# A written order of steps, moved up to batch 1's subtraction: where loads, maxima, transposes and query fetches stand

## The chip, the cores and the metric

The kernel runs on one core of a Trainium2 chip. Its time is the device time of one execution in microseconds (us); the time of a kernel is the median of its runs. Five engines run their own instruction streams in order and wait for each other through semaphores: TensorE (PE in the profile, with PEld for its weight loads), VectorE (DVE), ScalarE (ACT), GpSimd (POOL) and SyncE (SP), which here issues the DMAs.

## The reference, cut to what matters

Eight batches of 576 tokens pass through an attention over 32 memory slots (8 heads of 64) and then through a mixture of 8 experts in which each token goes to one expert:

```
a = exp(phi - max_tokens(phi));  a /= sum_tokens(a) + 1e-9
k_m = einsum('bhsm,bhsd->bhmd', a, k);  v_m = einsum('bhsm,bhsd->bhmd', a, v)
attn = softmax(q @ k_m.T / sqrt(64));   x = attn @ v_m        # 576 x 512 per batch
logits = x @ w_gate;  local = sigmoid(x @ w_local)
# token 0 takes its own best expert; a later token keeps its predecessor's
# expert e unless local < 0.5, then it takes its own best one
out = softmax(logits)[e] * (relu(x @ w1[e]) @ w2[e])          # w1 512 x 1024, w2 1024 x 512
```

## The kernel before

For each batch the expert of token 0 (the *choice*, L1023 to L1025) is found at run time, and this expert's W1 and W2 are loaded and applied to all 576 tokens; the few tokens that have another expert are done again in a loop at the end. The attention is folded into the expert's first layer: `x @ w1` is `at @ G`, where `at` are the attention weights (32 slots for each head, transposed, L986) and `G` is `kvT` times W1 (`pg`, L1220, split in a high and a low fp32r part `Gh`, L1233, and `Gl`, L1235). `at` is split in the same way into `ah` (L990) and `al` (L994). All products of the two expert layers are three fp32r products of such parts.

For each batch, PE runs `hidden` (L1251): 4 groups of 256 tokens and 8 groups of 320 tokens, each followed by ACT's relu (L1259) and DVE's remainder (L1260). Batch 0 then has `turned` (L1283 to L1285): four column blocks dc 0 to 3, each of 8 times three products, each block ended by DVE's transpose `oT` (L1288); two buffers `po` alternate. At last comes `natural` for the first 128 tokens (L1268 to L1270).

The order of everything else is a table written out by hand, `SCHEDULE`. Its first line runs before batch 0's expert layers; after that, one line is run at each `yield` of `hidden`, `turned` and `natural`. An entry "1 a qT 0" is the step "a qT 0" of batch 1; `STEPS` maps names to functions. Steps that the change moves:

- `phi`, `k`, `v` (L614), `q 0` and `q 1` (L640: queries of heads' first and second half, 8 DMAs each), `w1 ...` (L1185) and `w2 ...` (L1196): DMAs issued by SP, in program order. Eight semaphores go round, so an issue waits for the DMA eight issues earlier.
- `colmax` (L719) the maximum of `phi` over tokens as a tree of DVE operations, `pm`, `mc`, `pm2`, `cx` (L736 to L758) its last part over PE and ACT, `sub`, `dsub` (L763) the subtraction of it, `exp` (L767).
- for each part of the tokens (`p` and `z` of batch 0, `a` and `z` of batch 1): `qT` (L893, from `q_t`; batch 0 by PE, L912), `psc` (L925) the scores, `turn` (L938), `mx`, `sub`, `exp`, `sum` (L955 to L972), `inv`, `mul`, `at` (L976 to L986).
- `pl0` (L1010) the two products for the choice, `choice`, `expert` (SP reads the choice, L1424).
- `g lt` to `g prob` (L1045 to L1135): the gate of all tokens, small DVE operations.
- `warm`: products of zeros on PE, used by nothing.

Of the kernel before, what the change touches and what calls it, by code (L numbers as in the profile page):

```python
# [39 lines left out]
}  # L40

SCHEDULE = """
0 warm f, 0 phi 0, 0 colmax 0, 0 phi 1, 0 colmax 1, 0 kv tile, 0 q0 tile, 0 v 0, 0 k 0, 1 kv tile, 0 at, 0 k 1, 0 warm f, 0 warm f, 0 warm b, 0 v 1, 0 pm, 0 mc, 0 pm2, 0 cx, 0 dsub 0, 0 gate constants, 0 warm f, 0 warm f, 0 warm f, 0 warm f, 0 exp 0, 0 pkv a, 0 dsub 1, 0 warm b, 0 asum 0, 0 q0 a, 0 exp 1, 0 asum 1, 0 sums, 0 rinv, 0 pkv b, 0 kvn, 0 o q, 0 pT, 0 warm b, 0 warm b, 0 q0 b, 0 gate loads, 0 q0 c, 0 kvT, 0 o psc, 0 o turn, 0 o mx, 0 o sub, 0 o exp, 0 o sum, 0 o inv, 0 o mul, 0 gate turn, 0 p q 0, 0 p q 1 0, 0 pgg, 0 o at, 0 ggt, 0 p q 1 1, 0 pl0, 0 choice, 1 phi, 0 q0 d, 1 cm 0, 1 cm 1, 1 warm k, 0 p psc, 0 p turn, 2 phi, 0 p mx, 0 p sub 0, 0 p exp 0, 0 p sub 1, 1 cm 2, 0 p exp 1, 0 p sum 0, 1 warm v, 0 p sum 1, 0 p inv, 0 p mul 1, 0 z q 0, 0 z q 1, 0 expert, 0 z q 2, 0 w1 0 a, 1 pm, 1 mc, 0 p mul 0, 0 p at 0, 0 p ah 0, 0 w1 1 a, 0 pg lo, 0 Gh lo 0, 0 z psc, 0 w2 0, 0 z turn, 1 warm u, 0 warm b, 0 p at 1, 0 z mx, 1 v, 0 p al 0, 0 pg hi, 0 p ah 1, 0 p al 1, 0 Gh lo 1, 0 Gl lo, 0 z sub, 0 G hi, 1 pm2, 1 cx, 0 pg 1 lo, 0 G 1 lo, 0 z exp, 0 z sum
1 sub 1, 0 pg 1 hi, 1 exp 1, 0 z inv, 0 z mul, 0 z at, 0 G 1 hi, 0 split 0, 1 k, 0 z ah, 1 dsub 0, 0 w2 1

0 z al, 1 exp 0, 1 asum, 0 g pl

0 split 1, 0 split 2, 0 split 3
0 g lt

2 colmax, 1 pkv 0, 1 pkv 1, 1 sums, 1 rinv, 1 q 0, 0 g L, 0 split 4
0 split 5, 0 split 6

0 split 7, 1 q 1
1 kvn, 2 pm, 2 mc, 1 a qT 0

1 z qT 0, 0 g fresh, 0 g kept  # L60

1 pT, 2 pm2

2 cx
1 kvT, 1 z qT 1, 2 sub 1, 2 sub 0, 1 a qT 1, 1 a psc, 1 pgg, 1 a turn
1 a mx, 1 a sub  # L70


1 a exp

1 a sum
2 exp 0
2 kv, 0 g carry, 0 g exp, 0 g prob, 1 a inv

0 at store, 2 exp 1, 0 g cols, 0 gate 1, 1 a mul, 2 asum, 1 a at


# [392 lines left out]
def tile_memattn_stickymoe(  # L480
# [12 lines left out]
    nc = tc.nc  # L493
# [6 lines left out]
    NB = S // 32  # L500
# [88 lines left out]
    PB = 9  # L589
# [34 lines left out]
    def fetch_kv(st, which=(0, 1), piece=slice(0, TN)):  # L624

        if len(which) == 2:
            kv_tile(st)
        for i in which:
            load_tokens(st.kv[:, i], (k, v)[i][st.b], slice(0, HG), piece)

    def fetch_q(st, hs):

        if hs.start == 0:
            st.qt = pin.tile([P, HG, NB, 32], F32, tag="q", name="q_t", bufs=1)
        qv = q[st.b].rearrange("(h g) (i r) (j l) -> h g j r i l", g=NG, r=32, j=2)
# [46 lines left out]
    def warm(n, cols=512, own=True):  # L682

        if cols < 512 and own:
            wp = ps_o.tile([P, 512], F32, tag="po", name="wp")
        else:
            if not wt:
                wt[0] = ps_o.tile([P, 512], F32, tag="po", name="wp")
            wp = wt[0]
        for _ in range(n):  # L690
            if cols > 512:
                nc.tensor.matmul(wp, lhsT=zeros, rhs=zeros[:, 0:1].to_broadcast([P, 512]), start=True, stop=True)
                continue
            nc.tensor.matmul(wp[:, 0:cols], lhsT=wz[:, 0:P], rhs=wz[:, 0:cols], start=True, stop=True)
# [725 lines left out]
    a, z = PARTS  # L1420
# [21 lines left out]
    def al(st, p):  # L1442
# [4 lines left out]
    STEPS = {  # L1447

        "phi": lambda st: fetch_phi(st) if st.b > 1 else fetch_phi(st, False, pf, "oT"),
        "kv": fetch_kv,  # L1450
        "kv tile": kv_tile,
        "v": lambda st: fetch_kv(st, (1,)),
        "colmax": f_colmax,
        "pm": f_pm,
        "mc": f_mc,
# [174 lines left out]
    n = nc.values_load(cnt[0:1, 0:1], min_val=0, max_val=B * E)  # L1630
# [31 lines left out]
```

## Time and profile before

| what | value |
|---|---|
| median of 3 runs | 390.64 us (390.41, 390.64, 392.36) |
| profiled execution | 392.12 us, its span 390.3 us |
| PE busy | 382.3 us, 98% of the span |
| DVE, ACT, POOL busy | 285.2, 170.6, 157.3 us |
| mean granted TensorE clock | 0.993 of 2.4 GHz |
| first product of `hidden` | at 30.50 us |
| first `pl0` of batch 1 | at 69.02 us |

The span runs from the first to the last instruction; 1.8 us of the profiled execution lie outside of it. "Idle before <-X" in a row says how long an engine stood before that group and what released it.

### The profile page before, as it was taken

Reading aid. Unit: us, or ns where it says so; the run is one execution under the profiler, and the core shown is the slowest. Engines: PE = TensorE matmul, PEld = TensorE weight load, DVE = VectorE, ACT = ScalarE, POOL = GpSimd, SP = SyncE. Lnnn points to the kernel's source line nnn. Section 1 sums busy time; section 2 is a strip of 40 time slices with the busy share of each in tenths; the row PEclk is TensorE's granted clock in tenths of the full one; section 3 lists DMA queues with packets and bytes.
Section 4 is the critical chain, followed back from the end, with each engine's and each line's share of the span. In section 5 each row is a group of like instructions: output and inputs, shape, how many; then the busy total and the mean of one; then the engine's idle time right before and its main releaser. Section 6 shows DMA issues by size and latency. Waiting matters only on the chain. (4 is left out here: it accounts for less than half of the span.)

```text
span 390.3 us, 10303 instructions
## 1 busy us (share of the span) xinstructions
PE 382.3 (98%) x4088; PEld 329.8 (84%) x4088; DVE 285.2 (73%) x700; ACT 170.6 (44%) x430; POOL 157.3 (40%) x166
## 2 busy tenths in 40 slices
PE   8889999999999999999999999999999999999996
PEld 3658989789987998798987998879997998879995
DVE  4488769877968598666787788697896668765651
ACT  2337804276136641466205752357413753148111
POOL 1015940455026461457104673066304861336320
PEclk9989999999999999999999999999999999999999
DMA  7989798899729974997856389488797340584012
GB/s 232 265 285 395 139 265 176 268 351 325 142 101 329 268 171 179 349 304 141 273 215 225 114 165 314 135 322 226 127 359 294 123 109 16 183 267 179 0 36 91
DMA packets 119947, 82.55 MB, mean 211 GB/s; under 512 B 69972, under 2 KB 95320, under 8 KB 119896
## 3 DMA queue, kind: packets, MB, share of 16 engines
q1 hardware_dynamic: 119896, 81.86, 70.0%
q8 instruction: 33, 0.54, 0.6%
q14 instruction: 18, 0.15, 0.1%
HBM read 66.60 MB, written 15.24 MB: 210 GB/s over the span
## 5 line engine op out<-in xcount | busy, mean ns | idle before, releaser
L1208 POOL TENSOR_TENSOR w2l<-raw,w2h 128x512 fp32r<-128x512 f32 x64 | 81.4, 1298 | 49.0 <-ACT w2h L1207 28.4
L1283 PE MATMUL po<-h,w2l 128*128 128x448 f32 (+1 forms) x256 | 93.3, 365 | 0.0
L1285 PE MATMUL po<-h,w2h 128*128 128x448 f32 (+1 forms) x256 | 91.8, 359 | 0.0
L1284 PE MATMUL po<-h,w2h 128*128 128x448 f32 (+1 forms) x256 | 91.8, 359 | 0.0
L1260 DVE SCALAR_TENSOR_TENSOR h<-ph,h 128x320 fp32r<-128x320 f32 (+1 forms) x96 | 52.0, 553 | 32.5 <-ACT h L1259 32.0
L1251 PE MATMUL ph<-ah,Gh 128*128 128x256 f32 (+1 forms) x256 | 73.8, 303 | 0.0
L1251 PE MATMUL ph<-ah,Gl 128*128 128x256 f32 (+1 forms) x256 | 72.2, 296 | 0.0
L1294 POOL TENSOR_TENSOR oT<-oT,gT 128x448 f32<-128x448 f32 (+1 forms) x32 | 29.1, 925 | 85.0 <-ACT gT L1160 40.7
L1259 ACT ACTIVATE h<-ph 128x320 fp32r<-128x320 f32 (+1 forms) x96 | 46.3, 489 | 29.5 <-PE ph L1251 29.3
L1251 PE MATMUL ph<-al,Gh 128*128 128x256 f32 (+1 forms) x256 | 54.9, 295 | 0.0
L1251 PEld LDWEIGHTS ph<-ah,Gh 128*128 128x128 f32 x256 | 48.2, 188 | 4.3 <-issue 1.2
L1283 PEld LDWEIGHTS po<-h,w2l 128*128 128x128 f32 x256 | 48.3, 189 | 4.1 <-issue 0.7
L1285 PEld LDWEIGHTS po<-h,w2h 128*128 128x128 f32 x256 | 48.1, 188 | 3.6
L1284 PEld LDWEIGHTS po<-h,w2h 128*128 128x128 f32 x256 | 48.1, 188 | 3.2
L1251 PEld LDWEIGHTS ph<-ah,Gl 128*128 128x128 f32 x256 | 48.3, 189 | 0.4 <-DVE Gl L1235 0.2
L994 POOL TENSOR_TENSOR al<-at,ah 128x576 fp32r<-128x576 f32 (+1 forms) x18 | 23.7, 1319 | 44.4 <-ACT ah L990 44.2
L1251 PEld LDWEIGHTS ph<-al,Gh 128*128 128x128 f32 x256 | 41.1, 188 | 0.0
L1207 ACT ACTIVATE w2h<-raw 128x512 fp32r<-128x512 f32 x64 | 37.1, 626 | 0.1
L763 POOL TENSOR_TENSOR phi_t<-phi_t,cx 128x384 f32<-128x384 f32 (+1 forms) x13 | 18.5, 1436 | 41.5 <-ACT cx L758 30.0
L965 ACT ACTIVATE sc<-sc 128x576 f32<-128x576 f32 (+2 forms) x18 | 11.3, 631 | 47.6 <-DVE sc L960 47.6
L1268 PE MATMUL po<-w2h,h 128*128 128x512 f32 (+1 forms) x80 | 29.7, 371 | 0.0
L1269 PE MATMUL po<-w2l,h 128*128 128x512 f32 (+1 forms) x80 | 29.5, 369 | 0.0
(157 smaller groups left out, 555.9 us busy)
## 6 DMA issues: line engine op xcount, KB each, us to landing
raw<-in_moe_w_dram SPq DMA_DIRECT2D x34, 512.0 KB, 6.5
raw<-in_moe_w_dram SPq DMA_DIRECT2D x15, 1024.0 KB, 6.9
kv_t<-in_v_dram SPq DMA_DIRECT2D x7, 1152.0 KB, 9.3
kv_t<-in_k_dram SPq DMA_DIRECT2D x7, 1152.0 KB, 6.1
q_t<-in_q_dram SPq DMA_DIRECT2D x112, 72.0 KB, 2.9
out_dram<-oT SPq DMA_DIRECT2D x28, 224.0 KB, 4.0
att_d<-at SPq DMA_DIRECT2D x8, 576.0 KB, 5.7
phi_t<-in_phi_dram SPq DMA_DIRECT2D x7, 576.0 KB, 6.8
```

Source lines behind the costliest of these rows:

```text
L994: (eng or nc.gpsimd).tensor_tensor(out=st.al[:, gs, ss], in0=st.at[:, gs, ss], in1=st.ah[:, gs, ss], op=ALU.subtract)
L1207: nc.scalar.activation(h, src, AF.Copy)
L1208: nc.gpsimd.tensor_tensor(out=l, in0=src, in1=h, op=ALU.subtract)
L1251: nc.tensor.matmul(pv[:, c - c0], lhsT=lt[:, g, cs], rhs=rt[:, g, s0 : s0 + n], start=(i == 0), stop=(i == 5),)
L1259: nc.scalar.activation(hi, pv, AF.Relu)
L1260: nc.vector.scalar_tensor_tensor(out=lo, in0=pv, scalar=0.0, in1=hi, op0=ALU.max, op1=ALU.subtract)
L1268: nc.tensor.matmul(po, lhsT=ht[:, c, 0, ts], rhs=hi, start=(c == 0), stop=False)
L1269: nc.tensor.matmul(po, lhsT=ht[:, c, 0, ts], rhs=lo, start=False, stop=False)
L1283: nc.tensor.matmul(po[:, 0:n], lhsT=lo, rhs=ht[:, c, 0, s1:], start=(c == 0), stop=False)
L1284: nc.tensor.matmul(po[:, 0:n], lhsT=hi, rhs=ht[:, c, 0, s1:], start=False, stop=False)
L1285: nc.tensor.matmul(po[:, 0:n], lhsT=hi, rhs=ht[:, c, 1, s1:], start=False, stop=(c == FC - 1))
L1294: nc.gpsimd.tensor_tensor(out=x, in0=x, in1=g, op=ALU.mult)
```

## The change

The first line of the table and the lines up to the 41st yield are written anew; from the line "0 at store, ..." on, all is as it was. Two sets of fillers change (8 narrow products each instead of 39, 24 and 8), one drain of SP falls out, `ah` and `al` of part z are issued by halves, and the query tile is now made by whichever half is fetched first.

```diff
 SCHEDULE = """
...
-1 sub 1, 0 pg 1 hi, 1 exp 1, 0 z inv, 0 z mul, 0 z at, 0 G 1 hi, 0 split 0, 1 k, 0 z ah, 1 dsub 0, 0 w2 1
-
-0 z al, 1 exp 0, 1 asum, 0 g pl
-
-0 split 1, 0 split 2, 0 split 3
-0 g lt
-
-2 colmax, 1 pkv 0, 1 pkv 1, 1 sums, 1 rinv, 1 q 0, 0 g L, 0 split 4
-0 split 5, 0 split 6
-
-0 split 7, 1 q 1
-1 kvn, 2 pm, 2 mc, 1 a qT 0
...
-1 z qT 0, 0 g fresh, 0 g kept
...
-1 kvT, 1 z qT 1, 2 sub 1, 2 sub 0, 1 a qT 1, 1 a psc, 1 pgg, 1 a turn
-1 a mx, 1 a sub
...
+0 z exp, 0 z sum, 0 z inv, 1 exp 1, 1 exp 0, 1 asum, 0 pg 1 hi, 0 G 1 hi, 0 z mul, 0 z at
+0 z ah 0, 0 z al 0
+0 z ah 1, 0 z al 1
+0 w2 0, 0 split 0, 1 pkv 0, 1 pkv 1, 0 split 1, 0 split 2, 0 split 3, 2 colmax, 1 sums, 0 g pl
+
+0 w2 1, 0 split 4
+0 split 5
+1 q 1, 1 q 0
...
+1 a qT 0, 1 z qT 0
...
+2 pm2, 1 a qT 1, 2 cx, 0 g fresh, 0 g kept, 1 pT, 1 kvT
+
+0 g carry, 0 g exp, 0 g prob
...
+1 z qT 1
...
+1 a psc, 2 sub 0, 1 a turn, 1 a mx, 1 a sub, 1 a exp, 1 a sum, 1 pgg
...
-        if hs.start == 0:
+        if not hasattr(st, "qt"):
             st.qt = pin.tile([P, HG, NB, 32], F32, tag="q", name="q_t", bufs=1)
...
-        "idle": lambda st: [nc.sync.drain(), nc.sync.drain()],
-        "warm u": lambda st: warm(39, 32, False),
-        "warm k": lambda st: warm(24, 32, False),
-        "warm v": lambda st: warm(8, 32, False),
+        "idle": lambda st: nc.sync.drain(),
+        "warm n": lambda st: warm(8, 32, False),
...
+        STEPS[f"z ah {g}"] = lambda st, g=g: k_ah(st, PB, NB, each[g])
+        STEPS[f"z al {g}"] = lambda st, g=g: k_al(st, PB, NB, gs=each[g])
```

On SP, the rows from the last load that is issued ahead of the choice to the queries now stand as follows (`ei` is the choice that SP reads; `raw` are the loads of W1, L1185, and of W2, L1196; rows that repeat one above them, and those in which SP works out an address, are left out).

```order
L614 DMA phi_t<-in_phi_dram 128x4x288
L614 DMA kv_t<-in_k_dram 128x4x576
L1424 TENSOR_LOAD ei
L1185 DMA raw_513<-in_moe_w_dram 128x4x256
L1185 DMA raw_516<-in_moe_w_dram 128x4x256
L614 DMA phi_t<-in_phi_dram 128x4x288
L614 DMA kv_t<-in_v_dram 128x4x576
L1196 DMA raw_684<-in_moe_w_dram 128x2x512
L1196 DMA raw_814<-in_moe_w_dram 128x2x512
L640 DMA q_t<-in_q_dram 32x18x32 x16
```

Before, the second `phi` load stood ahead of the choice, the two halves of W1 and the first half of W2 behind it, and then `v`, `k`, the second half of W2 and the queries; the 16 query DMAs came with the first half of the heads first, now the second half comes first.

On DVE around the choice of batch 0, the rows of the difference are these (`m` and `ei` are the choice's, `sc<-psc` the transposes of part p's scores, `tree` batch 1's maxima).

```order
 L986 STREAM_TRANSPOSE at<-sc 128x2x32
-L1023 MAX m_357<-pl_354 1x8
-L1024 MAX_INDEX ei<-m_357,pl_354 1x8
+L938 STREAM_TRANSPOSE sc<-psc 128x256 x2
+L1023 MAX m_372<-pl_369 1x8
+L1024 MAX_INDEX ei<-m_372,pl_369 1x8
 L1025 TENSOR_SCALAR c_0_118<-ei 1x1
-L719 TENSOR_TENSOR tree<-phi_t 128x512
-L719 TENSOR_TENSOR tree<-tree 128x4x64
-L938 STREAM_TRANSPOSE sc<-psc 128x256 x2
 L955 TENSOR_REDUCE mx<-sc 128x16
```

The transposes of part p moved ahead of the choice, and the tree behind it. Further on, DVE came to `G`'s remainders straight after part z's maxima; now these rows stand there:

```order
L986 STREAM_TRANSPOSE at<-sc 128x256
L763 TENSOR_TENSOR phi_t<-phi_t,cx 128x4x192
L955 TENSOR_REDUCE mx<-sc 128x18
L1235 TENSOR_TENSOR Gl<-pg,Gh 128x256 x6
L960 TENSOR_TENSOR sc<-sc,mx 128x576
```

The first subtraction of batch 1 (L763) came in ahead of them; before, it stood behind the last of the `Gl`.

On DVE in the stage of `turned` of batch 0, these rows stood in a row before (from the maxima of batch 2, L740, over the transposes of batch 1's queries, L893, to the gate, L1064 to L1072).

```order
L740 TENSOR_REDUCE mc<-pm 128x2
L893 STREAM_TRANSPOSE qT<-q_t 128x576 x2
L1064 TENSOR_REDUCE gmx<-L 32x18
L1066 TENSOR_TENSOR ex<-L,gmx 32x144
L1068 SCALAR_TENSOR_TENSOR t_950<-ex,code 32x144
```

Now three of the four transposes stand there:

```order
L740 TENSOR_REDUCE mc<-pm 128x2
L893 STREAM_TRANSPOSE qT<-q_t 128x576 x3
L1064 TENSOR_REDUCE gmx<-L 32x18
L1066 TENSOR_TENSOR ex<-L,gmx 32x144
L1068 SCALAR_TENSOR_TENSOR t_961<-ex,code 32x144
```

The first two of them are of the first half of the heads, in both orders; the third came over from behind the gate's first part. The fourth now comes behind the gate's later part (L1104 to L1135), on the same engine:

```order
L1134 TENSOR_REDUCE pe<-ex 32x18
L1135 TENSOR_TENSOR pr<-pe,es_1000 32x18
L893 STREAM_TRANSPOSE qT<-q_t 128x576
L1288 STREAM_TRANSPOSE oT<-po 128x14x32
L938 STREAM_TRANSPOSE sc<-psc 128x288 x2
```

Before, that later part stood between the scores' sum (L972) and L976; now it stands ahead of the scores' transposes (L938).

## Rows read from the trace of the kernel before

**Rows 1.** The page: its first line.
```profile
span 390.3 us, 10303 instructions
```
**Rows 2.** Windows by stage: busy time and count of each engine, clock, DMA share, GB/s.
```profile
30.50:47.50 17.00, 17.00 (x298) 15.85 (x290) 13.53 (x29) 13.45 (x31) 13.36 (x13) 1.00 0.91 269
47.50:69.00 21.50, 21.50 (x136) 19.17 (x134) 17.55 (x47) 6.59 (x23) 6.63 (x6) 1.00 0.91 213
```
**Rows 3.** Timeline of PE before the first product of `hidden`: start, duration, what.
```profile
24.73 0.30 PE L736 MATMUL pm<-ident,cm 128*128 128x128 f32 x1 [1.46 <-DVE cm L719]
...
26.65 1.64 PE L694 MATMUL wp<-wz 128*128 128x32 bf16 x40
28.22 1.23 PE L1220 MATMUL pg<-raw,kvT 64*32 64x256 f32 x16
...
30.50 0.39 PE L1251 MATMUL ph<-ah,Gh 128*128 128x256 f32 x1
```
**Rows 4.** Windows around the low clock; columns as in rows 2.
```profile
20.00:23.30 3.30, 3.27 (x65) 2.51 (x61) 2.63 (x7) 0.00 (x0) 0.00 (x0) 1.00 0.80 249
23.30:26.70 3.40, 1.97 (x35) 0.87 (x36) 3.26 (x11) 2.19 (x6) 0.00 (x0) 1.00 0.89 299
26.70:30.10 3.40, 3.40 (x68) 1.84 (x73) 3.37 (x9) 2.05 (x8) 1.59 (x2) 0.50 0.95 316
30.10:33.50 3.40, 3.40 (x50) 2.45 (x35) 2.94 (x8) 2.75 (x9) 1.01 (x1) 1.00 1.05 398
```
**Rows 5.** Timeline of DVE from the choice to the first subtraction.
```profile
19.46 0.16 DVE L1023 MAX8 m<-pl 1x8 f32<-1x8 f32 x1 [0.43 <-PE pl L1010]
...
19.99 0.14 DVE L1025 TENSOR_SCALAR c<-ei 1x1 f32<-1x1 uint32 x1
20.70 0.69 DVE L719 TENSOR_TENSOR tree<-phi_t 128x512 f32<-128x512 f32 x1 [0.56 <-DMA phi_t<-in_phi_dram]
...
21.77 0.77 DVE L938 STREAM_TRANSPOSE sc<-psc 128x256 f32<-128x256 f32 x2
...
28.82 0.74 DVE L1235 TENSOR_TENSOR Gl<-pg,Gh 128x256 fp32r<-128x256 f32 x2
...
36.11 0.94 DVE L763 TENSOR_TENSOR phi_t<-phi_t,cx 128x768 f32<-128x768 f32 x1
```
**Rows 6.** Line L1185, batch 0's loads of W1: from issue to landing.
```profile
DMA to landing us min/median/max: 4.4/5.0/6.5
```
**Rows 7.** Timeline of SP: batch 1's query DMAs, first issue and time of all issues.
```profile
31.19 18.66 SPq L640 DMA_DIRECT2D q_t<-in_q_dram  x16
```
**Rows 8.** DMA issues from 49.3 to 49.9: count, size, median us to landing.
```profile
q_t<-in_q_dram SPq DMA_DIRECT2D x2, 72.0 KB, 4.1
```
**Rows 9.** Timeline of DVE in the stage of `turned`.
```profile
48.73 1.43 DVE L893 STREAM_TRANSPOSE qT<-q_t 128x576 f32<-128x576 f32 x2
...
52.70 0.65 DVE L1288 STREAM_TRANSPOSE oT<-po 128x448 f32<-128x448 f32 x1 [0.19 <-PE po L1285]
...
57.30 0.85 DVE L938 STREAM_TRANSPOSE sc<-psc 128x288 f32<-128x288 f32 x2 [2.53 <-PE pgg L866]
...
58.97 0.76 DVE L960 TENSOR_TENSOR sc<-sc,mx 128x576 f32<-128x576 f32 x1
...
60.48 0.75 DVE L972 TENSOR_REDUCE sm<-sc 128x18 f32<-128x576 f32 x1 [0.19 <-ACT sc L965]
61.15 0.22 DVE L1104 STREAM_TRANSPOSE endt<-end 32x64 f32<-32x64 f32 x1
...
63.95 0.16 DVE L976 TENSOR_SCALAR sm<-sm 128x18 f32<-128x18 f32 x1
...
67.78 0.75 DVE L986 STREAM_TRANSPOSE at<-sc 128x576 f32<-128x576 f32 x1
```
**Rows 10.** Timeline of PE: part a's scores, and the products of batch 1's choice.
```profile
56.50 0.71 PE L925 MATMUL psc<-qT,kvT 64*32 64x288 f32 x16
...
69.02 0.24 PE L1010 MATMUL pl<-ggt,at 128*1 128x8 f32 x4
```

More of the change, by code (lines that the diff above doesn't have):

```diff
@@ L42 @@
 SCHEDULE = """
-0 warm f, 0 phi 0, 0 colmax 0, 0 phi 1, 0 colmax 1, 0 kv tile, 0 q0 tile, 0 v 0, 0 k 0, 1 kv tile, 0 at, 0 k 1, 0 warm f, 0 warm f, 0 warm b, 0 v 1, 0 pm, 0 mc, 0 pm2, 0 cx, 0 dsub 0, 0 gate constants, 0 warm f, 0 warm f, 0 warm f, 0 warm f, 0 exp 0, 0 pkv a, 0 dsub 1, 0 warm b, 0 asum 0, 0 q0 a, 0 exp 1, 0 asum 1, 0 sums, 0 rinv, 0 pkv b, 0 kvn, 0 o q, 0 pT, 0 warm b, 0 warm b, 0 q0 b, 0 gate loads, 0 q0 c, 0 kvT, 0 o psc, 0 o turn, 0 o mx, 0 o sub, 0 o exp, 0 o sum, 0 o inv, 0 o mul, 0 gate turn, 0 p q 0, 0 p q 1 0, 0 pgg, 0 o at, 0 ggt, 0 p q 1 1, 0 pl0, 0 choice, 1 phi, 0 q0 d, 1 cm 0, 1 cm 1, 1 warm k, 0 p psc, 0 p turn, 2 phi, 0 p mx, 0 p sub 0, 0 p exp 0, 0 p sub 1, 1 cm 2, 0 p exp 1, 0 p sum 0, 1 warm v, 0 p sum 1, 0 p inv, 0 p mul 1, 0 z q 0, 0 z q 1, 0 expert, 0 z q 2, 0 w1 0 a, 1 pm, 1 mc, 0 p mul 0, 0 p at 0, 0 p ah 0, 0 w1 1 a, 0 pg lo, 0 Gh lo 0, 0 z psc, 0 w2 0, 0 z turn, 1 warm u, 0 warm b, 0 p at 1, 0 z mx, 1 v, 0 p al 0, 0 pg hi, 0 p ah 1, 0 p al 1, 0 Gh lo 1, 0 Gl lo, 0 z sub, 0 G hi, 1 pm2, 1 cx, 0 pg 1 lo, 0 G 1 lo, 0 z exp, 0 z sum
@@ L44 @@
-1 sub 1, 0 pg 1 hi, 1 exp 1, 0 z inv, 0 z mul, 0 z at, 0 G 1 hi, 0 split 0, 1 k, 0 z ah, 1 dsub 0, 0 w2 1
-0 z al, 1 exp 0, 1 asum, 0 g pl
-0 split 1, 0 split 2, 0 split 3
-0 g lt
-2 colmax, 1 pkv 0, 1 pkv 1, 1 sums, 1 rinv, 1 q 0, 0 g L, 0 split 4
-0 split 5, 0 split 6
-0 split 7, 1 q 1
-1 kvn, 2 pm, 2 mc, 1 a qT 0
-1 z qT 0, 0 g fresh, 0 g kept
-1 pT, 2 pm2
-2 cx
-1 kvT, 1 z qT 1, 2 sub 1, 2 sub 0, 1 a qT 1, 1 a psc, 1 pgg, 1 a turn
-1 a mx, 1 a sub
-1 a exp
-1 a sum
+0 warm f, 0 phi 0, 0 colmax 0, 0 phi 1, 0 colmax 1, 0 kv tile, 0 q0 tile, 0 v 0, 0 k 0, 1 kv tile, 0 at, 0 k 1, 0 warm f, 0 warm f, 0 warm b, 0 v 1, 0 pm, 0 mc, 0 pm2, 0 cx, 0 dsub 0, 0 gate constants, 0 warm f, 0 warm f, 0 warm f, 0 warm f, 0 exp 0, 0 pkv a, 0 dsub 1, 0 warm b, 0 asum 0, 0 q0 a, 0 exp 1, 0 asum 1, 0 sums, 0 rinv, 0 pkv b, 0 kvn, 0 o q, 0 pT, 0 warm b, 0 warm b, 0 q0 b, 0 gate loads, 0 kvT, 0 o psc, 0 o turn, 0 o mx, 0 o sub, 0 q0 c, 0 o exp, 0 q0 d, 0 o sum, 0 o inv, 0 p q 0, 0 o mul, 0 gate turn, 0 p q 1 0, 0 p q 1 1, 0 pgg, 0 ggt, 0 o at, 0 p psc, 0 p turn, 0 pl0, 0 choice, 0 warm n, 0 warm n, 0 warm n, 0 warm n, 1 phi, 0 p mx, 0 p sub 0, 0 p exp 0, 0 z q 0, 0 warm n, 0 p sub 1, 0 p exp 1, 0 z q 1, 0 warm n, 0 warm n, 0 warm n, 0 warm b, 0 z q 2, 1 cm 0, 0 p sum 0, 1 cm 1, 0 warm b, 0 p sum 1, 1 cm 2, 1 pm, 0 z psc, 0 p inv, 1 k, 1 mc, 1 pm2, 1 cx, 0 expert, 0 w1 0 a, 0 w1 1 a, 0 pg lo, 0 Gh lo 1, 0 p mul 0, 0 p at 0, 0 p ah 0, 2 phi, 0 p mul 1, 0 z turn, 0 p at 1, 0 warm b, 0 p al 0, 0 warm b, 0 warm b, 0 warm b, 1 sub 1, 0 warm b, 1 dsub 0, 0 p ah 1, 0 p al 1, 0 warm b, 1 v, 0 Gh lo 0, 0 z mx, 0 Gl lo, 0 warm b, 0 warm b, 0 pg hi, 0 G hi, 0 pg 1 lo, 0 G 1 lo, 0 z sub
@@ new lines @@
+0 z exp, 0 z sum, 0 z inv, 1 exp 1, 1 exp 0, 1 asum, 0 pg 1 hi, 0 G 1 hi, 0 z mul, 0 z at
[5 more added lines that the diff above has]
+1 q 1, 1 q 0
+0 g lt, 0 split 6, 0 split 7, 1 rinv, 1 kvn
+2 pm
+2 mc
+0 g L
+1 a qT 0, 1 z qT 0
[3 more added lines that the diff above has]
+1 a psc, 2 sub 0, 1 a turn, 1 a mx, 1 a sub, 1 a exp, 1 a sum, 1 pgg
@@ L76 @@
+2 sub 1
 2 exp 0
-2 kv, 0 g carry, 0 g exp, 0 g prob, 1 a inv
+2 kv, 1 a inv
 0 at store, 2 exp 1, 0 g cols, 0 gate 1, 1 a mul, 2 asum, 1 a at
```

## The prediction

> **What bounds the kernel now.** I read the windows by stage first. From 30.50 to 69.00 us PE is busy for all of it, 17.00 of 17.00 and 21.50 of 21.50 us [rows 2]: from the first product of `hidden` on, nothing but PE's own work sets the end, and a product that starts later, or a wait inside this stretch, moves the end by its full length. So two places decide what a new order is worth: when the first product starts, and whether PE is made to wait behind it. The timeline of PE ahead of 30.50 shows the first place [rows 3]: PE stood 1.46 us for batch 1's maximum `cm` before 24.73, then came 40 fillers (1.64 us) and 16 products of `pg` that took 1.23 us. The windows say why these were long: PE was busy for only 1.97 of 3.40 us between 23.30 and 26.70, and in the next 3.40 us the granted clock was 0.50, its lower level of 1.2 GHz; then it was 1.00 again [rows 4]. The second place is the choice of batch 1: its products on PE stood at 69.02 [rows 10], behind DVE's `at`, which ended at 67.78 + 0.75 = 68.53 [rows 9].
>
> **The first product.** What is removed and added on DVE ahead of it: part p's transposes (0.77 us) only change places with the choice, which began at 19.46 and ended at 19.99 + 0.14 = 20.13 [rows 5], 0.67 us long. As the transposes now need part p's scores, I let them begin at about 20.1, when before the choice had ended, and the choice at 20.9, 1.4 us later than before. From 20.70 to the end of the first two `Gl` (28.82 + 0.74 = 29.56) DVE worked almost without a stop for 8.86 us, those transposes included. Now it does the same from 20.1, and the choice (0.67) and the subtraction L763 (0.94) with it: 20.1 + 8.86 + 0.67 + 0.94 = 30.6 for the second `Gl`, 30.2 for the first. The first product needs only `Gh`, the second the first `Gl`. So PE can begin at 30.0 to 30.5 instead of 30.50, if its own chain is no longer: PE's stand of 1.46 us is spread out, since `cm` now comes between sums and fillers lie around it, and its `pg` at full clock would be half as long. A gain of 0 to 0.5 us, at most a loss of 0.7 if the choice comes at 21.6.
>
> The loads: SP reads the choice some 1.4 us later, with `k` of batch 1 (1152 KB) queued ahead of W1. At the 398 GB/s of the best window [rows 4] `k` takes 3.0 us; behind the `phi` load that landed at 20.70 [rows 5] it is in by about 23.7, and the first part of W1 (512 KB, 1.3 us) by 25.0 to 25.6, where before it took 4.4 us from its issue at the least [rows 6] and landed at 25.0. PE needs it only after the maxima's last products, which DVE's order puts at about 26.7 (an estimate: `cm` and `mc` lie behind the choice and some 4 us of other work). I cost this at nothing; without that cover it is 0.6 us. The DMA engines were busy for 0.80 and 0.89 of 20.00 to 26.70 [rows 4], which leaves 0.66 + 0.37 = 1.0 us that `k` can fill: later transfers come up to 1.0 us sooner. `v`, the second `phi` and W2 only change places in the same queue.
>
> **The queries.** This is the term that I take to decide. The 16 query DMAs were issued from 31.19 to 49.85, the last at about 49.4 [rows 7], and the last two took 4.1 us (median) to land [rows 8]: X = 53.4. Before, DVE's first two transposes of them (the first half of heads, fetched first) started at 48.73 [rows 9] with half of the queries still on their way. Now the half that they need is fetched second, so the first transpose waits for the last landing: X is 53.4, or 52.4 where the 1.0 us above comes back whole. Behind the waiting transpose stand all of DVE: the gate, `oT` of block 0 (for which PE waits with block 2), the scores and `at`. What DVE has to do from the first transpose to the end of `at` is the same set as before: 48.73 to 68.53 is 19.80 us, less its stands of 0.19, 2.53 and 0.19 us [rows 9], so 16.9 us of work. One stand is added: the scores' sum waits for ACT's exponentials, from 58.97 + 0.76 = 59.73 to 60.48 before, 0.75 us, in which an `oT` was done that now comes behind. So `at` ends at X + 17.6 and batch 1's `pl0` on PE stands at X + 17.7: 71.1 for X = 53.4, 70.1 for 52.4, against 69.02. PE, which has only its own order, stands for the difference: 1.1 to 2.1 us. Against this DVE's old stand of 2.53 us ahead of part a's scores is gone, already in the sum. I take 1.7 us, as the spacing of the last issues rather than the early queue sets X, and 0 to 0.3 us for batch 1's choice and W1 that follow. A first product that starts 0.5 us earlier gives nothing here: it is X that sets this place.
>
> **Against which time.** The profiled execution took 392.12 us, 1.8 us beyond its span of 390.3 us [rows 1], and lies 1.48 us above the median of 390.64; one run of three (392.36) lies with it, two (390.41 and 390.64) lower. The stretch at the lower clock explains this at least in part: the fillers and `pg` in it, 1.64 + 1.23 us [rows 3], would take half, 1.4 us less. If so, X stays where it is and the sum is 392.12 + 1.7 = 393.8; if the distance lies elsewhere, 390.64 + 1.7 = 392.3. I forecast 393.5, nearer to the first, with 392.3 to 394.5 for this case.
>
> The Trainium skill (TensorE: Matmul & The Clock Gate, The HAM clock gate) says that throttling is the default, that activity releases it, and that the window it is judged by is free-running, so that the same kernel can meet it at another phase from run to run. Rows 4 agree as far as they go (a half-idle stretch, then the lower clock); no row here shows two runs side by side. By that rule the order with less idle time on PE would lose its slow runs, and with no wait at the queries it would come out at some 390.6 us in every run, which is rival B below on the median's footing.
>
> **The rivals.**
> *B, the queries come in time (not slower).* If the fillings of the queue bring X to 51.4 or less, 2 us sooner than the rows say, PE does not stand. Then part a's scores decide: they stood at 56.50 [rows 10] and move behind 15 more products of block 2 (the stage has 96 of them in 21.50 us [rows 2], 0.20 to 0.22 each), about 3.0 us, to 59.5; their transposes begin at 60.2, and what follows on DVE before was 68.53 − 57.30 = 11.2 us, less the gate's part from 61.15 to 63.95, 2.8 us [rows 9], so 68.6 + 0.3, and `pl0` keeps its place. The time would be 392.12 less 0 to 0.5, 391.6 to 392.1, or on the median's footing 390.6; 391.5 stands for it. For it speaks that the queue carries the same bytes and has 1.0 us to win; against it, that the DMAs' issue alone ended at 49.85.
> *C, the lower clock comes again (slower).* PE's stand of 1.7 us at `pl0` is longer than the 1.46 us after which the clock fell in rows 3 and 4. A stretch of 3.40 us at 0.50 inside the products would cost 1.7 us more: 395.3. Against it: PE is otherwise full around 69 us, as it was not at 23.30 to 26.70.
> *D, the first product starts much sooner.* If DVE is not the bound that I work out, `pg` at full clock lets PE start at 29.1 instead of 30.50; with B's prompt queries that is 390.7, and below 388.7 only if the start came 3.4 us sooner, ahead of any `Gl`.
>
> **How the numbers follow.** 0.5% of 390.64 is 1.95 us, about what a measurement of this kernel tells from no change: under 388.7 is faster, above 392.6 slower. The forecast has a chance of 0.58, B 0.22, C 0.08, D 0.12. Slower: 0.50 of the forecast's 0.58 (the part that is not on the median's footing), 0.08 of C, 0.02 of B, 0.60 together. Faster: 0.03 of D. Same: the rest, 0.37. The range runs from 390.9 (in B's and D's middle) to 394.7 (the forecast's upper end and a little of C) and leaves out about 2 in 10.
>
> **What would show it.** Right: in the timeline of DVE a stand of about 4 us ahead of the first L893 of batch 1, released by the query DMA, with its start at 52 to 53.5; a stand of PE at L1010 near 70 us of 1 to 2 us; the first L1251 between 30.0 and 30.6; clock 1.00 from 20 us on; W1 landed before `pg` wants it. Wrong: the first L893 below 51.4, no idle time of PE before L1010, a first L1251 under 29.5, or a window at 0.50 behind 30 us.

## The result and the profile after

The changed kernel takes 393.47 us (median of 15 runs, 392.84 to 397.35), the kernel before, run beside it, 391.46 us (390.39 to 392.69). The ratio is 1.0056 with a 95% interval of 1.004 to 1.0072: slower by about 2.2 us. The profiled execution took 393.51 us with a span of 391.6 us, so again some 1.9 us lie outside the span.

The windows by stage answer to [rows 2], the next three to [rows 4] (busy time and count of PE, PEld, DVE, ACT and POOL, then clock, DMA share, GB/s):

```profile
30.50:47.50 17.00, 16.75 (x288) 15.60 (x288) 13.41 (x27) 12.60 (x30) 13.18 (x14) 1.00 0.93 265
47.50:69.00 21.50, 21.50 (x138) 19.40 (x136) 17.05 (x46) 7.06 (x26) 6.47 (x6) 1.00 0.73 192
69.00:80.40 11.40, 10.70 (x253) 7.65 (x251) 8.83 (x24) 4.00 (x8) 4.12 (x4) 1.00 0.95 286
...
20.00:23.30 3.30, 3.14 (x83) 2.50 (x69) 2.67 (x10) 0.42 (x2) 0.00 (x0) 1.00 0.67 256
23.30:26.70 3.40, 3.33 (x62) 2.04 (x58) 3.20 (x11) 1.99 (x5) 0.00 (x0) 1.00 0.98 316
26.70:30.10 3.40, 3.40 (x53) 1.41 (x56) 3.40 (x9) 1.80 (x6) 1.79 (x2) 1.00 1.00 318
```

PE has no hole ahead of the first product any more (3.33 of 3.40 us busy, where it was 1.97) and the clock stays at 1.00. But PE now stands inside the products: 0.25 us in the first stage and 0.70 us behind 69.00, where it had stood for nothing. The timeline of PE names both places; the rows of 30.43 and 70.02 answer to the last rows of [rows 3] and [rows 10].

```profile
26.45 0.33 PE L749 MATMUL pm<-ident,mcw 128*128 128x128 f32 x1
26.71 0.66 PE L1220 MATMUL pg<-raw,kvT 64*32 64x256 f32 x16
27.31 1.90 PE L694 MATMUL wp<-wz 128*128 128x512 bf16 x8
29.14 1.36 PE L1220 MATMUL pg<-raw,kvT 64*32 64x256 f32 x32
30.43 0.38 PE L1251 MATMUL ph<-ah,Gh 128*128 128x256 f32 x1
...
31.53 0.38 PE L1251 MATMUL ph<-al,Gh 128*128 128x256 f32 x1 [0.25 <-POOL al L994]
...
70.02 0.24 PE L1010 MATMUL pl<-ggt,at 128*1 128x8 f32 x4 [0.69 <-DVE at L986]
```

The timeline of DVE shows why PE stood at L1010; the first row answers to the first of [rows 9]:

```profile
52.02 2.10 DVE L893 STREAM_TRANSPOSE qT<-q_t 128x576 f32<-128x576 f32 x3 [2.63 <-DMA q_t<-in_q_dram]
54.04 0.25 DVE L1064 TENSOR_REDUCE gmx<-L 32x18 f32<-32x144 f32 x1
54.32 0.77 DVE L1066 TENSOR_TENSOR ex<-L,gmx 32x144 f32<-32x144 f32 x1
...
61.43 0.79 DVE L938 STREAM_TRANSPOSE sc<-psc 128x288 f32<-128x288 f32 x2
...
64.56 0.75 DVE L972 TENSOR_REDUCE sm<-sc 128x18 f32<-128x576 f32 x1 [0.75 <-ACT sc L965]
...
69.11 0.77 DVE L986 STREAM_TRANSPOSE at<-sc 128x576 f32<-128x576 f32 x1
```

DVE stood 2.63 us for the last query, began at 52.02, and from there ran without a stop but for the 0.75 us of the exponentials: `at` ends at 69.88, 17.86 us behind, and PE's products for batch 1's choice come at 70.02 instead of 69.02.

**The same kernel before, at full clock.** The rows ahead of the prediction were those of an execution with a stretch at half the clock. One more profile of the unchanged kernel had none. Its timeline of PE and its windows:

```profile
26.42 1.37 PE L694 MATMUL wp<-wz 128*128 128x32 bf16 x40
27.72 0.79 PE L1220 MATMUL pg<-raw,kvT 64*32 64x256 f32 x16
28.44 0.33 PE L749 MATMUL pm<-ident,mcw 128*128 128x128 f32 x1
28.85 0.67 PE L1220 MATMUL pg<-raw,kvT 64*32 64x256 f32 x16
29.45 0.38 PE L1251 MATMUL ph<-ah,Gh 128*128 128x256 f32 x1
...
67.97 0.24 PE L1010 MATMUL pl<-ggt,at 128*1 128x8 f32 x4
...
23.30:26.70 3.40, 2.17 (x48) 1.30 (x49) 3.23 (x12) 2.23 (x6) 0.00 (x0) 1.00 0.91 303
26.70:30.10 3.40, 3.32 (x74) 2.10 (x71) 3.40 (x9) 2.65 (x9) 2.12 (x3) 1.00 1.08 390
```

It was nearly as idle between 23.30 and 26.70 (2.17 us busy, where [rows 4] have 1.97), yet its clock stayed; the `pg` behind the fillers took 0.79 us where [rows 3] have 1.23, the first product stood at 29.45 instead of 30.50, and the time was 390.8 instead of 392.12 us. Against this execution the changed one is 0.98 us later at the first product and 2.05 us later at L1010: 0.98 of late start, 0.25 for `al`, 0.69 at L1010 itself, and 0.13 in small shares between. These are shares of PE's time. They do not say what each cause would cost alone: by DVE's rows above `at` ends at 69.88 whatever PE does, so a punctual first product would have made the stand at L1010 longer, and L1010 no earlier.

### The profile page after: what moved, and what is told of

It is laid out like the page before. It is cut to its first block, busy times and chain, and to the rows that moved or that the text cites. A ratio compares the mean times of both kernels' runs of the same rounds, so it can differ in the third digit from the quotient of the medians.

```text
span 391.6 us, 10305 instructions
## 1 busy us (share of the span) xinstructions
PE 383.7 (98%) x4090; PEld 329.9 (84%) x4090; DVE 285.3 (73%) x700; ACT 170.5 (44%) x431; POOL 157.4 (40%) x166
## 5 line engine op out<-in xcount | busy, mean ns | idle before, releaser
L763 POOL TENSOR_TENSOR phi_t<-phi_t,cx 128x384 f32<-128x384 f32 (+1 forms) x13 | 18.6, 1438 | 37.9 <-ACT cx L758 26.4
L1268 PE MATMUL po<-w2h,h 128*128 128x512 f32 (+1 forms) x80 | 29.7, 371 | 0.0
```

The costliest lines, as they stand in the source:

```text
L1268: nc.tensor.matmul(po, lhsT=ht[:, c, 0, ts], rhs=hi, start=(c == 0), stop=False)
```

## The experiments

The theory Q is that of the prediction: the late half of the queries holds DVE, and through it PE. The rival H is that the new order ahead of the first product costs the time. All ratios are to the kernel before, run beside each, with 95% intervals.

| kernel | median us | before us | ratio | first product us | L1010 us |
|---|---|---|---|---|---|
| changed | 393.47 | 391.46 | 1.0056 (1.004 to 1.0072) | 30.43 | 70.02 |
| e1 half first | 392.86 | 391.02 | 1.004 (1.0027 to 1.0054) | 30.21 | 69.09 |
| e2 half last | 395.18 | 391.02 | 1.0089 (1.0059 to 1.0118) | 29.22 | 72.38 |
| e3 new head | 395.05 | 391.02 | 1.0086 (1.0068 to 1.0104) | 30.64 | 72.08 |
| e4 new tail | 395.73 | 391.02 | 1.0122 (1.0103 to 1.014) | 29.59 | 71.73 |
| e5 filled | 392.09 | 391.13 | 1.0024 (1.0012 to 1.0036) | 28.86 | 67.54 |
| e6 W1 | 394.18 | 391.13 | 1.0087 (1.0059 to 1.0115) | 29.98 | 70.34 |
| e7 al | 392.29 | 391.13 | 1.0032 (1.002 to 1.0043) | 29.85 | 68.68 |
| e8 both | 393.37 | 391.13 | 1.006 (1.0042 to 1.0078) | 29.50 | 69.75 |
| e9 filled even | 390.94 | 391.16 | 0.9995 (0.9981 to 1.0009) | 29.27 | 68.15 |
| e10 later qT | 392.30 | 391.16 | 1.0033 (1.0021 to 1.0046) | 31.31 | 69.76 |
| before again | 390.80 | 391.16 | one run | 29.45 | 67.97 |
| e11 head back | 391.80 | 391.75 | 1.0006 (0.9993 to 1.0018) | 28.91 | 68.21 |

The last two columns are of the one profiled execution of each. Such a place differs by up to 0.8 us between executions: the copy of `kvT` on DVE (L854), which comes ahead of the choice, stood at 15.4 to 16.3 us. So the first product is also given as a distance behind this copy.

**e1, the first half first.** The two fetches of the changed kernel change back.

```diff
-1 q 1, 1 q 0
+1 q 0, 1 q 1
```

> The changed order with the two query fetches changed back (first half of the heads first). Theory Q (the late half of the queries holds DVE, and through it PE at batch 1's choice): DVE's first transpose of batch 1's queries starts near 49.4 us, only the third waits for the last landing near 52 us, so that DVE is some 1.35 us ahead of the changed kernel, PE's stand of 0.69 us at L1010 is gone, and the time falls by 0.7 to 1.2 us, to about 392.5. Rival H (the new order ahead of the first product costs the time, the queries little): the time stays at 393.5 within 0.3 us.

In PE's timeline the stand at L1010 is gone, the one for `al` is not:

```profile
31.37 0.39 PE L1251 MATMUL ph<-al,Gh 128*128 128x256 f32 x1 [0.30 <-POOL al L994]
...
69.09 0.24 PE L1010 MATMUL pl<-ggt,at 128*1 128x8 f32 x4
```

L1010 comes 0.93 us sooner, as Q says. The ratio falls only from 1.0056 to 1.004, 0.6 us, with intervals that overlap: Q holds for its place, and leaves about 1.6 us that it doesn't explain. So both theories have a share, and the shares overlap: with the queries in time, L1010 still waits for PE's own late start.

**e2, the half alone.** The kernel before with the fetches the other way round (and the query tile made by whichever comes first, as in the change).

```diff
-2 colmax, 1 pkv 0, 1 pkv 1, 1 sums, 1 rinv, 1 q 0, 0 g L, 0 split 4
+2 colmax, 1 pkv 0, 1 pkv 1, 1 sums, 1 rinv, 1 q 1, 0 g L, 0 split 4
...
-0 split 7, 1 q 1
+0 split 7, 1 q 0
```

> The kernel before with nothing changed but the two query fetches: the second half of the heads first. Theory Q: DVE's first transpose waits for the last landing at 52 to 53.4 us instead of 48.73, L1010 comes at 69.7 to 71.0 behind a stand of PE, and the time rises by 0.7 to 2.0 us over before, to 392.2 to 393.4. Rival H: within 0.3 us of before, since the old order of the scores and the gate leaves DVE a stand of 2.5 us to give.

The first timeline row is of DVE, the two behind it are of PE, and the two windows have the columns of [rows 4]:

```profile
51.81 1.44 DVE L893 STREAM_TRANSPOSE qT<-q_t 128x576 f32<-128x576 f32 x2 [4.10 <-DMA q_t<-in_q_dram]
...
56.31 0.30 PE L749 MATMUL pm<-ident,mcw 128*128 128x128 f32 x1 [2.79 <-DVE oT L1288]
...
72.38 0.24 PE L1010 MATMUL pl<-ggt,at 128*1 128x8 f32 x4
...
57.60:58.00 0.40, 0.40 (x4) 0.34 (x3) 0.00 (x0) 0.00 (x0) 0.40 (x2) 0.73 0.98 403
58.00:61.00 3.00, 3.00 (x38) 1.82 (x37) 0.85 (x2) 0.00 (x0) 1.78 (x2) 0.50 0.89 210
```

The landing is where Q puts it (51.81), the price is more than it said: 0.0089 of 391.02 is 3.5 us. PE stood earlier than I thought, at 56.31, released by DVE's first `oT`, which waits behind the query transposes; and after the stand of 2.79 us the granted clock fell to 0.50. That is rival C of the prediction, seen in another kernel than the one it was written for. The low clock is not the whole price: two of the nine runs had a mean clock of 1.0, and they took 393.57 and 394.88 us.

**e3 and e4, head and tail apart.** The first line of one table with lines 1 to 41 of the other, each step once. e3 has the new first line and then the old lines, of which the first becomes this:

```diff
-1 sub 1, 0 pg 1 hi, 1 exp 1, 0 z inv, 0 z mul, 0 z at, 0 G 1 hi, 0 split 0, 1 k, 0 z ah, 1 dsub 0, 0 w2 1
+0 w2 0, 0 z exp, 0 z sum, 0 pg 1 hi, 1 exp 1, 0 z inv, 0 z mul, 0 z at, 0 G 1 hi, 0 split 0, 0 z ah, 0 w2 1
```

e4 has the old first line and then the new lines, of which the first and the fourth become these:

```diff
-0 z exp, 0 z sum, 0 z inv, 1 exp 1, 1 exp 0, 1 asum, 0 pg 1 hi, 0 G 1 hi, 0 z mul, 0 z at
+1 k, 1 sub 1, 1 dsub 0, 0 z inv, 1 exp 1, 1 exp 0, 1 asum, 0 pg 1 hi, 0 G 1 hi, 0 z mul, 0 z at
...
-0 w2 0, 0 split 0, 1 pkv 0, 1 pkv 1, 0 split 1, 0 split 2, 0 split 3, 2 colmax, 1 sums, 0 g pl
+0 split 0, 1 pkv 0, 1 pkv 1, 0 split 1, 0 split 2, 0 split 3, 2 colmax, 1 sums, 0 g pl
```

> The changed order up to the first product, and from there the old order up to the 41st yield (steps that the new first line has already done are left out of it; W2's first half and part z's exponentials and sum, which the old first line had, stand at the first yield). Theory Q: no stand at L1010, the time of before, 391.0 to 391.7. Rival H: the head alone costs some 1 us or more, 392.4 to 393.5.

> The old order up to the first product, and the new one behind it (with batch 1's keys and subtraction, which the new first line held, at the first yield). Theory Q: DVE waits for the last query at about 52 to 53 us and PE stands at L1010 as in the changed kernel; 392.2 to 393.5. Rival H: the time of before, 391.0 to 391.7.

Both are slower than either whole kernel, so the expectations of both theories fell for both. There are new stands, here one of e3 and then one of e4, from their timelines of PE; they make up only a part of the loss:

```profile
40.25 0.41 PE L1251 MATMUL ph<-ah,Gh 128*128 128x320 f32 x1 [0.92 <-DVE h L1260]
```

```profile
38.47 3.85 PE L794 MATMUL pkv<-kv_t,phi_t 64*32 64x128 f32 x144 [1.40 <-DMA kv_t<-in_k_dram]
```

What e4 tells is that the new lines take batch 1's keys sooner than the old place of their load lets them land: the fetch ahead of the choice belongs to the products at the fourth yield. As a way to share out the 2.2 us the pair is inconclusive.

**e5, the hole filled.** The kernel before with seven fillers where PE stood for `cm`.

```diff
-0 w1 0 a, 1 pm, 1 mc,
+0 w1 0 a, 0 warm b, 0 warm b, 0 warm b, 0 warm b, 0 warm b, 0 warm b, 0 warm b, 1 pm, 1 mc,
```

> The kernel before with seven 512-column fillers on PE in the 1.46 us in which it stood for batch 1's maximum, and nothing else. Theory H (before, at full clock, starts the first product about 1 us sooner than its profiled execution showed, and the changed order lost that): the granted clock is 1.00 from 20 us on in every run, the first product stands at 29.0 to 29.8 us instead of 30.50, and the runs that showed a mean clock of 0.996 and 391.4 to 392.2 us fall away, so that the median is 390.2 to 390.8. Rival: the clock has nothing to do with the spread of the times; the first product stays at 30.5 us or the median stays at 391.0 with the same spread.

No run of it has a mean clock under 0.998, and the first product is at 28.86, 13.11 us behind the copy of `kvT` and a little ahead of the expected range. But the median is 0.96 us over before's. Its timeline of PE has two stands that no engine ended:

```profile
28.86 0.39 PE L1251 MATMUL ph<-ah,Gh 128*128 128x256 f32 x1
...
126.19 0.28 PE L1251 MATMUL ph<-ah,Gh 128*128 128x256 f32 x1 [0.27 <-issue]
...
225.45 0.41 PE L1251 MATMUL ph<-ah,Gh 128*128 128x320 f32 x1 [0.69 <-issue]
```

The clock's part of H is right; the time's was not.

**e6, e7, e8, three edits on e1.** e6 takes W1's delay back (the choice ahead of part p's scores, batch 1's keys behind W1), e7 `al`'s, e8 both. The first three pairs of lines are e6, the last is e7.

```diff
-0 o at, 0 p psc, 0 p turn, 0 pl0, 0 choice,
+0 o at, 0 pl0, 0 choice, 0 p psc, 0 p turn,
...
-0 p inv, 1 k, 1 mc,
+0 p inv, 1 mc,
...
-0 w1 1 a, 0 pg lo,
+0 w1 1 a, 1 k, 0 pg lo,
...
-1 sub 1, 0 warm b, 1 dsub 0, 0 p ah 1, 0 p al 1,
+0 warm b, 1 dsub 0, 0 p ah 1, 0 p al 1, 1 sub 1,
```

> The first variant (changed order, first half of queries first) with the choice ahead of part p's scores and transposes again, and batch 1's keys behind the four loads of W1. Theory H says that the third quarter of W1, which landed at 29.7 us in the changed kernel and feeds the last pg ahead of the first product, is one of two bounds of the start: it lands 1.0 to 1.7 us sooner, the first product stands at 29.8 to 30.2 instead of 30.4, but PE then waits 0.6 to 1.0 us for GpSimd's second al, so the time stays within 0.3 us of the first variant's 392.9. Rival: W1 alone decides, and the time falls by 0.7 us or more.

> The first variant with batch 1's subtraction on GpSimd behind the second al of part p instead of ahead of it. Theory H: the wait of 0.30 us for al behind the first product goes, the first product stays at 30.3 to 30.5 us as W1 bounds it, and the time falls by 0.2 to 0.4 us against the first variant's 392.9. Rival: al does not matter, or its wait turns into one for Gl, and the time stays.

> Both of these edits on the first variant. Theory H: with W1 and al both in time the first product stands at 29.7 to 30.0 us, bounded by DVE's Gl behind batch 1's subtraction, without a wait behind it, and the time falls by 0.6 to 1.0 us against the first variant's 392.9, to about 392.0. Rival: something else in the head (DVE alone) bounds the start, and the time stays within 0.4 us of 392.9.

GpSimd in the changed kernel had done batch 1's subtraction between the two halves of `al`; in e7 both halves come first (timelines of POOL, the changed kernel and e7):

```profile
28.31 1.45 POOL L994 TENSOR_TENSOR al<-at,ah 128x288 fp32r<-128x288 f32 x1 [25.71 <-ACT ah L990]
29.72 0.99 POOL L763 TENSOR_TENSOR phi_t<-phi_t,cx 128x384 f32<-128x384 f32 x1
30.68 0.80 POOL L994 TENSOR_TENSOR al<-at,ah 128x288 fp32r<-128x288 f32 x1
```

```profile
27.87 2.22 POOL L994 TENSOR_TENSOR al<-at,ah 128x288 fp32r<-128x288 f32 x2 [25.27 <-ACT ah L990]
30.04 1.03 POOL L763 TENSOR_TENSOR phi_t<-phi_t,cx 128x384 f32<-128x384 f32 x1
```

The wait of 0.30 us is gone in e7 and the ratio is 1.0032 instead of 1.004, in the direction and size expected, but within the intervals. e6 and e8 are slower, not faster: with the keys behind W1, PE stood for the products of batch 1's keys and values. First e8's timeline of PE, then how long the load of the values, issued at 24.4 us, took to land:

```profile
37.63 2.22 PE L794 MATMUL pkv<-kv_t,phi_t 64*32 64x128 f32 x143 [1.34 <-issue]
...
L614 SPq DMA_DIRECT2D kv_t<-in_v_dram x1: 2051/2051/2051, 24.4 to 24.4; - x1
...
DMA to landing us min/median/max: 13.1/13.1/13.1
```

No engine is named there, but the values landed at 37.5 and the products began at 37.63 (in e6 at 37.9 and 37.98); the keys had landed at 33.0. In the changed kernel the values landed at 35.9, ahead of the products at 37.66. Both kernels have a stand at L1010 again, 0.70 us in e6 and 0.46 in e8, behind DVE's `at`. Behind the copy of `kvT` the first product came at 14.38 us (changed), 14.33 (e1), 14.23 (e7), 14.08 (e6) and 14.09 (e8): taking W1's lateness back, and that of the choice with it, gains 0.1 to 0.3 us there, not the 1 us and more by which W1 lands sooner. In all of these PE's row before the first product is full; what fills it are the eight wide fillers of 1.90 us.

**e9, the hole filled evenly.** e5 with the narrow fillers behind the hole cut by as many.

```diff
-        "warm u": lambda st: warm(39, 32, False),
+        "warm u": lambda st: warm(32, 32, False),
```

> The kernel before with the seven fillers in PE's stand for batch 1's maximum, as in the filled one, but with seven of the 39 narrow fillers behind them taken out, so that PE's stream has as many instructions as before. Theory: the filled kernel won 1.6 us up to batch 1 and lost 1.0 us of it again in stands of PE at 126 and 225 us that no engine ended, because its later instructions stood elsewhere in the stream; with the count unchanged these stands are gone, the granted clock stays at 1.00 from 20 us on, and the median is 390.2 to 390.7, with no run of a mean clock under 0.998. Rival: the stands come with the earlier start itself; they stay, and the median is 391.5 or more.

The window of the earlier hole is full and the clock is up, and there is no stand "issue":

```profile
23.30:26.70 3.40, 3.39 (x52) 1.45 (x51) 3.23 (x12) 2.23 (x6) 0.00 (x0) 1.00 0.82 238
26.70:30.10 3.40, 3.27 (x67) 2.05 (x64) 3.40 (x9) 2.79 (x10) 2.16 (x3) 1.00 1.05 380
```

None of 12 runs had a mean clock under 0.998, against 5 of 20 of before's beside it (0.993 to 0.996, 391.35 to 392.47 us). The median is 390.94, above the 390.2 to 390.7 that I expected, and the ratio cannot be told from 1: the filling takes away the low clock, but its other runs still spread from 390.04 to 391.72 us.

**e10, the third transpose later.** e7 with DVE's order of [rows 9] at this point.

```diff
-2 pm2, 1 a qT 1, 2 cx, 0 g fresh, 0 g kept, 1 pT, 1 kvT
+2 pm2, 2 cx, 0 g fresh, 0 g kept, 1 a qT 1, 1 pT, 1 kvT
```

> The seventh kernel (changed order, first half of queries first, al ahead of batch 1's subtraction) with DVE's third query transpose behind the gate's first part, as in the order before. Theory Q: DVE no longer waits for the last query at all, the stand of PE of 0.43 us at L1010 goes, and the time falls by 0.3 to 0.6 us against 392.3, to 391.7 to 392.0. Rival: the stand at L1010 comes from the gate standing ahead of the scores; it stays, and so does the time.

L1010 had a stand of 0.43 us in e7 and has none here, but the time did not fall, 392.30 against 392.29. The profiled execution lost time at another place, a stand of 0.62 us ahead of a filler at 24.89 that no engine ended, and a first product at 31.31, as W1's third part landed only at 30.6. I count it as inconclusive on the time and as a yes for the stand.

> The kernel before, unchanged, once more. Theory H: most of its runs have a mean clock of 1.0, so most likely no stretch at 0.50 here; then the first product stands 13.5 to 13.7 us behind the copy of kvT at 15.6 to 16.0 us (L854), at about 29.4 us instead of 30.50, and the time is 390.4 to 391.0. If the stretch comes again, 30.5 us and 391.4 to 392.4.

This is the execution shown under the result; it came out as the first case says (13.2 us behind the copy, 390.8 us).

**e11, all of it back.** e10 with the choice ahead of part p's scores, batch 1's subtraction on DVE behind the `Gl`, and four of the eight fillers out. The keys stay ahead of the choice.

```diff
-0 o at, 0 p psc, 0 p turn, 0 pl0, 0 choice,
+0 o at, 0 pl0, 0 choice, 0 p psc, 0 p turn,
...
-0 p al 0, 0 warm b, 0 warm b, 0 warm b, 0 warm b, 1 dsub 0, 0 p ah 1,
+0 p al 0, 0 warm b, 0 p ah 1,
...
-0 Gl lo, 0 warm b, 0 warm b, 0 pg hi, 0 G hi, 0 pg 1 lo, 0 G 1 lo, 0 z sub
+0 Gl lo, 0 warm b, 0 pg hi, 0 G hi, 0 pg 1 lo, 0 G 1 lo, 1 dsub 0, 0 z sub
```

> The tenth kernel (changed order, first half of queries first, al ahead of batch 1's subtraction, third query transpose behind the gate's first part) with the head's other three delays taken back: the choice ahead of part p's scores and transposes, DVE's subtraction of batch 1 behind the six Gl, and four of the eight wide fillers ahead of the second pg out; batch 1's keys stay ahead of the choice. Theory (late start plus late query, nothing else): the first product stands 13.2 to 13.7 us behind the copy of kvT (L854), as in the kernel before at full clock (13.2) and not 14.4 as in the changed one, PE stands at L1010 for 0.4 us at most, and the time is that of before within 0.5 us, 390.7 to 391.7. Rival: the changed order costs something further on that the timelines do not name; the time stays at 392.0 or more.

```profile
26.20 0.66 PE L1220 MATMUL pg<-raw,kvT 64*32 64x256 f32 x16
26.80 1.04 PE L694 MATMUL wp<-wz 128*128 128x512 bf16 x4
27.76 1.22 PE L1220 MATMUL pg<-raw,kvT 64*32 64x256 f32 x32
28.91 0.39 PE L1251 MATMUL ph<-ah,Gh 128*128 128x256 f32 x1
...
68.21 0.24 PE L1010 MATMUL pl<-ggt,at 128*1 128x8 f32 x4
```

In these rows of PE the first product stands at 28.91, 13.22 us behind the copy of `kvT`, and L1010 has no wait worth naming. The ratio is 1.0006 (0.9993 to 1.0018): with the late start and the late query taken back, most of the slowdown is gone, though most of the new order is still in it. That is what the theory asked for. It is not proof of nothing left: 8 of the 17 runs of the kernel before beside it had a mean clock under 0.998, and none of e11's. Against the other nine, with a median of 391.28 us, e11 is 0.5 us slower, which their spread (390.49 to 392.45) can't tell from nothing; and its trace has 39.30 us from the first product to L1010, in small shares longer than the 38.52 of the kernel before again. So the rival, a cost further on, is excluded only above about 1 us.

## Why the prediction was right

**The total** was forecast as 393.5 and came out at 393.47, within the range and on the side that had most of the chance. That they agree to 0.03 us is luck. Against the profiled execution of the kernel before, the changed one is 1.00 us later at L1010 and 0.39 us more behind it, 1.39 together; the sum had 1.7, and the forecast took 0.3 off because the baseline was in doubt. The baseline moved, too: the rise forecast over the 390.64 of three runs was 2.9 us, the median of 15 runs is 391.46, and the rise is 2.2 us by the ratio.

**The queries** held DVE and PE as the prediction put it: first L893 at 52.02 (forecast 52.4 to 53.4), released by the query DMA, `at` 17.86 us behind it (17.6), a stand of PE at L1010. The mis-sized term is X, 0.4 to 1.4 us sooner than I took it, so that L1010 came 1.00 us later than in [rows 10], not 1.7. It was not the 1.0 us that `k` fills which came back: SP issued the queries from 31.02 to 49.70 us, only 0.15 us sooner at the end than in [rows 7]. DVE's first transpose began at 52.02, so the last of them landed at most 2.8 us behind its issue at 49.2, where I had taken the 4.1 us of [rows 8], the landing of a single DMA. Two signs came out smaller than named, DVE's stand (2.63 us, not about 4) and PE's (0.69 us, not 1 to 2), the second because PE itself was late. That an earlier first product gives nothing at this place fits the rows: `at` ends where the queries put it. e1 and e2 show the mechanism from both sides; in the old order the same swap costs 3.5 us, since there the first `oT` stands behind the transposes and PE's stand brought the low clock, in the profiled execution and in most of the others.

**The first product** stood at 30.43, inside the 30.0 to 30.5 that DVE's sum gave. DVE's sum itself came out well, its first `Gl` ended at about 30.0 (forecast 30.2), but it did not set the start; W1 and PE's own row did, as shown below, so the number is in part luck. Nor is it the gain that this seemed to be: against the same kernel at full clock it is 0.98 us late. The part "Against which time" had said so, by halving the fillers and `pg` of [rows 3], which gave 1.4 us; the kernel before again shows 1.05 us at the first product and 1.32 us in the time. Over the 79 runs of the kernel before that ran beside the experiments it is less: 23 had a mean clock under 0.998, with a median of 391.87 us, the other 56 have 390.96, so the low clock is worth about 0.9 us. That same part decided the forecast by its choice of baseline: from the median of 390.64 it would have been 392.3.

**The step that failed is W1 and `al` at no cost.** The rows are right that W1's first part comes in time. I did not look at the third ("W1 landed before `pg` wants it" was one of the signs of being right), which feeds the last 16 products of `pg` ahead of the first product. It was issued at 23.4 us and landed at 29.7; in the kernel before again it was issued at 23.3 and landed at 28.7. The third load and the weight loads (PEld) of that `pg`, first in the changed kernel and then in the kernel before again:

```profile
L1185 SPq DMA_DIRECT2D raw<-in_moe_w_dram x1: 373/373/373, 23.4 to 23.4; - x1
...
DMA to landing us min/median/max: 6.3/6.3/6.3
...
29.80 0.21 PEld L1220 LDWEIGHTS pg<-raw,kvT 64*32 64x32 f32 x16 [0.36 <-DVE mx L955]
```

```profile
L1185 SPq DMA_DIRECT2D raw<-in_moe_w_dram x1: 373/373/373, 23.3 to 23.3; - x1
...
DMA to landing us min/median/max: 5.4/5.4/5.4
...
28.82 0.21 PEld L1220 LDWEIGHTS pg<-raw,kvT 64*32 64x32 f32 x16 [0.25 <-DVE mx L955]
```

The rows name DVE's maxima, but it is the load: in these two and in e1, e3 and e10 this `pg` began 0.1 us behind the landing each time, while the maxima ended anywhere from 0.3 us ahead of it to just behind it (in e10 they ended at 30.36, the load landed at 30.6 and the `pg` began at 30.68). The two landings differ by 1.0 us, the two first products by 0.98: W1 is the late start as it stands. It is worth only 0.1 to 0.3 us by e6 and e8 because the next bound is close. PE's own row would have let this `pg` begin only 0.14 us sooner (32 products in 1.36 us, in e11 in 1.22), and in that row four of the wide fillers make 0.86 us (1.90 against 1.04 in e11). The prediction put no price on these fillers. e11 took both bounds back together. And batch 1's subtraction on GpSimd, moved ahead of the second `al`, is not in the prediction at all: 0.25 us.

**The clock** was 1.00 from 20 us on, as forecast, and the low clock explains a part of the spread of before's runs; e9 shows that filling the hole removes it. The Trainium skill (TensorE: Matmul & The Clock Gate, The HAM clock gate) has the clock judged over a free-running window, so that one kernel can meet it differently from run to run; the two executions of the kernel before agree, as far as two can, with 1.97 us busy and then 0.50, and 2.17 us busy and then 1.00. Rival C did not come true in the changed kernel's profiled execution, whose stand at L1010 was 0.69 us, nor in 13 others of its 15 runs, with a mean clock of 0.998 or more; one run took 397.35 us at a mean clock of 0.994, and no trace shows where it lost the clock. Rivals B and D are excluded by the rows of 52.02 and 30.43. Of the 2.6 us between the spans of the changed kernel (391.6) and the kernel before again (389.0), 2.05 are at L1010; the remaining 0.5 us behind it, in single executions, stay unexplained.

## What to carry to other kernels

When one engine is full from some point on, a new order is priced at two places only: the start of the full stretch, and each wait inside it, where every moved step on the waiting engine's suppliers counts, GpSimd's small ones too. A transpose that waits for a DMA holds all that stands behind it on its engine, so which half is fetched first has to follow the order of use. Two waits that meet at one place don't add up: the later one hides the other, and taking back one alone gains only the distance to the next, as e1, e6 and e8 did. And before a profile is used as the baseline, its own time is set against the other runs: here one stretch at a lower clock hid a late start of 1 us.

## What the runs showed of the hardware that was not expected

With seven more fillers near 24 us PE had two stands, 0.27 us at 126 and 0.69 us at 225 us, for which no engine or DMA is named, and the median rose by 0.96 us (e5); with the count of PE's instructions as before (e9) the stands were gone. What the stands are is not shown. The same kernel with the same hole, 1.97 and 2.17 us busy of 3.40, fell to the lower clock in one execution and not in another. After PE's stand of 2.79 us in e2, PE first ran at 1.00 from 56.31 on, and the granted clock fell to 0.50 only some 1.5 us behind the end of the stand, between 57.60 (1.00 ahead of it) and 58.00.
